# Weights, transposed tokens and tokens by segment laid out on the host, with the layout steps on the chip taken out, in a gated mix of recurrent and local attention

## The chip, the core and the metric

The kernel runs on one core of a Trainium2 chip. The engines named here are PE (TensorE: matrix products; its weight loads are listed apart as PEld), DVE (VectorE), ACT (ScalarE), POOL (GpSimd) and SP (SyncE, which here only issues DMAs; "SPq" and "ACTq" are the queues in which SP and ACT issue them). The metric is the device time of one execution in microseconds, as the median of three runs.

## The reference

The output is a mix of two attentions over the same 2048 tokens of width 640: A is recurrent over 64 segments of 32 tokens, B is local with a window of 8 keys at every second position. All tensors are bf16.

```python
# A: 32 heads of 192, 8 memory tokens, 64 segments of 32 tokens
mem = mem0
for s in range(64):
    h = concatenate([mem, x[:, 32 * s:32 * s + 32]], axis=1)          # 40 tokens
    q, k, v = (einsum('btd,dhe->bhte', h, W) for W in (Wq, Wk, Wv))
    p = softmax(where(mask, q @ k.T * 192 ** -0.5, -1e9))             # causal over the segment, memory open
    o = einsum('bhte,hed->btd', p @ v, Wo)
    mem, a_s = o[:, :8], o[:, 8:]
a = concatenate(a_s)
# B: 32 heads of 20; position t sees t, t-2, ..., t-14
q, k, v = split(x @ wqkv);  b = softmax(q . k_window * 20 ** -0.5) @ v_window @ wo
g = sigmoid((x * gate_w).sum(-1))
out = g * a + (1 - g) * b
```

[...]

## The kernel before

The program has four stages, one after the other.

*Part B* (`part_b`, L87) computes B and the gate g for all tokens and leaves (1 - g) * B in `bsc_dram`. Tokens are in sixteen tiles of 128. `load_x` brings a tile in as rows (ACT issues the first four, POOL the others), `make_xT` (L158) transposes four tiles on PE against an identity (L163; 80 of these, and five more for the memory tokens), copies them from PSUM with DVE or ACT, computes the gate of the four tiles, and has POOL build two more layouts of the same tokens: `xh_blk` (each segment's transposed tokens with the last eight first) and `zx_blk` (the last eight tokens of each segment). `store_blocks` (L200) writes them to `xh_dram` and `zT_dram`, which the later stages read.

The attention of B runs over five blocks of up to 484 tokens and eight head groups of four heads. For each block `proj` (L236) projects q and k in ten chunks of 128 columns and stores each to DRAM (L248), and `load_qk` (L250) loads them back in eight loads with the heads on the partitions that the score products need (the tiles bqT and bkT; 20 rows for each head at partitions 0, 32, 64 and 96). `scores` (L258) and `values` (L280) do a step of one block and one head group. `store_ot` (L303) and `load_ot` (L310) take the block's result (OT) through DRAM again, from 20 rows a head in 32-partition places to dense rows (OTc), for `out_tile` (L318), which multiplies by wo. While a step of one block runs, `fill` gives PE the next block's projections, V products and transposes and the out tiles of the block before, by the lists in `plans`. The last three out tiles are "padded": head groups 6 and 7 are taken from OT as it stands, with a copy of wo that has zero rows in the 12 unused places of each head (`wop`), so that they needn't go through DRAM.

The order of PE, ACT, DVE and SP in this stage is written out by hand (`manual_schedule`). SP issues nearly every DMA. Between the loads and stores of B it issues, by `fetch` (L352), two lists of work for the later stages, one or two entries at a step: first `load_early` (L523) for 13 slices of A's weights that stay on chip, then `copy_scratch` (L527) for 21 half slices that are streamed later: these go from the weight inputs to scratch tensors `wscr` in DRAM, in the order in which the stream needs each row. `sources` (L451) gives the pieces of a slice: a half slice of Wq or Wk is 64 of each 128 columns, a slice of Wv comes in two pieces, one of Wo in rows of 384 or 256 columns.

[...]

*The pre-pass* (`prepass`, L598) computes q, k and v of the last eight tokens of each segment, through all of A's weights, into `zpk_dram`. It loads zT (L609, on ACT's queue) and POOL makes a second layout of it, zTi (L610). Then 48 chunks of q and 48 of k (L621, five products each), for which `get_columns` loads the columns that aren't on chip into the seven slots `wst` (L594), and three rounds of V (L652). `load_late(0)` loads slices of k into place at the beginning of the stage (`wlate_k`, L520, on SP), and some of v at chunks 8 and 17 of k. The results are copied from PSUM by ACT and DVE (ZS, ZV) and stored in rows of some 256 bytes.

*Part A* (`part_a`, L701) is the recurrence: 64 segments, most in a loop. In each, 21 half slices (5 MB) are streamed from `wscr` into the seven slots by `pump` (L553), in the order of `STREAM`, and the other slices are resident.

*The tail* (`part_z`, L1170) makes the last output rows.

`weights_setup` (L500) sorts the slices that are not streamed: the first N_EARLY, which are q slices, are loaded in part B, those after them up to LATE0 bytes a partition in `load_late(0)`, the rest in `load_late(1)`.

Of the kernel before, what the change touches and what calls it, by code (L numbers as in the profile page):

```python
# [15 lines left out]
N_EARLY = 13  # L16
N_LAST = 7
LATE0 = 84992
# [5 lines left out]

def _ap(base, dims):
    return bass.AP(tensor=base.tensor, offset=base.offset, ap=[list(base.ap[0])] + [list(d) for d in dims])

class _K:

    def __init__(self, ctx, tc, A_x, A_mem0, A_Wq, A_Wk, A_Wv, A_Wo, seg_len, B_wqkv, B_wo, gate_w, out):  # L30
# [56 lines left out]
    def part_b(self):  # L87
# [6 lines left out]
        self.zT_dram = self.dram.tile([128, KC, S // 32, 8], BF, name="zT_dram")  # L94
        self.oz_dram = [self.dram.tile([S // 32, 128, 192], BF, name=f"oz_dram{h}") for h in range(2)]
        g_dram = self.dram.tile([4, 32, self.NT], F32, name="g_dram")
        self.xh_dram = self.dram.tile([S // 32, 128, KC * 32], BF, name="xh_dram")
        self.gZ = self.const.tile([128, 4], F32, name="gZ")
        with ExitStack() as ctx:
            wp = ctx.enter_context(tc.tile_pool(name="b_w", bufs=1))  # L100
            io = ctx.enter_context(tc.tile_pool(name="b_io", bufs=4))
            blkp = ctx.enter_context(tc.tile_pool(name="b_blk", bufs=1))
# [8 lines left out]
            self.build_ident(wp)  # L111
            xs = {}

            def load_x(i):
                xs[i] = io.tile([128, 640], BF, name="x_sb")
                (nc.scalar if i < 4 else nc.gpsimd).dma_start(xs[i][:], self.x2d[i * 128:(i + 1) * 128, :])

            for i in range(4):
                load_x(i)
            mem = wp.tile([128, 640], BF, name="mem_sb")  # L120
            nc.vector.memset(mem[:], 0.0)
            nc.sync.dma_start(mem[0:8, :], self.mem0)
# [3 lines left out]
            wqk = [wp.tile([128, KC, 640], BF, name=f"w{n}_sb") for n in "qk"]  # L126
# [4 lines left out]
            wsrc = self.wqkv.rearrange("(c p) f -> p c f", p=128)  # L131
            for n, w in enumerate(wqk):
                (nc.scalar, nc.sync)[n].dma_start(w[:], wsrc[:, :, 640 * n:640 * n + 640])
            nc.sync.dma_start(gw[:], self.gate_w.rearrange("(c p o) -> p c o", p=128, o=1))
            nc.scalar.dma_start(wv[:], wsrc[:, :, 1280:1920])
            nc.sync.dma_start(woc[:], self.wo.rearrange("(c p) f -> p c f", p=128))
            wop = wp.tile([128, 2, 640], BF, name="wo_pad")
            nc.gpsimd.memset(wop[:], 0.0)
            for hh in range(4):
                nc.sync.dma_start(wop[32 * hh:32 * hh + 20], self.wo[480:640].rearrange("(g h d) f -> h d g f", g=2, h=4)[hh])  # L140
# [17 lines left out]
            def make_xT(b, kcs=range(KC)):  # L158
                t0 = 512 * b
                for kc in kcs:  # L160
                    ps = bank(BF, "ps_xT")
                    for i in range(4):
                        nc.tensor.transpose(ps[:, i * 128:(i + 1) * 128], xs[4 * b + i][:, kc * 128:(kc + 1) * 128],  # L163
                                            self.ident[:])
                    self.evac(xT[:, kc, HALO + t0:HALO + t0 + 512], ps[:, 0:512], "act" if b < 2 and kc % 2 else "dve")
                if kcs[-1] < KC - 1:
                    return
                for i in range(4):
                    del xs[4 * b + i]
                    if 4 * b + 4 + i < self.NT:  # L170
                        load_x(4 * b + 4 + i)
# [12 lines left out]
                xv = xT[:, :, HALO + t0:HALO + t0 + 512].rearrange("p c (s t) -> p s c t", t=32)  # L184
                xh = blkp.tile([128, 16, KC, 32], BF, name="xh_blk")
                nc.gpsimd.tensor_copy(xh[:, :, :, 8:32], xv[:, :, :, 0:24])
                s0 = int(b == 0)
                nc.gpsimd.tensor_copy(xh[:, s0:, :, 0:8], xv[:, s0:, :, 24:32])
                if b == 0:
                    ps = bank(BF, "ps_mT")  # L190
                    for kc in range(KC):
                        nc.tensor.transpose(ps[:, kc * 128:(kc + 1) * 128], mem[:, kc * 128:(kc + 1) * 128], self.ident[:])
                    nc.vector.tensor_copy(xh[:, 0, :, 0:8], ps[:, 0:640].rearrange("p (c i) -> p c i", i=128)[:, :, 0:8])
                zx = blkp.tile([128, KC, 16, 8], BF, name="zx_blk")
                nc.gpsimd.tensor_copy(zx[:].rearrange("p c s i -> p s c i"), xv[:, :, :, 24:32])
                blocks[b] = xh, zx

            blocks = {}

            def store_blocks(b):  # L200
                xh, zx = blocks.pop(b)
                self.first_store = nc.sync.dma_start(self.xh_dram[16 * b:16 * b + 16].rearrange("s p f -> p s f"),
                                  xh[:].rearrange("p s c t -> p s (c t)")).ins
                nc.sync.dma_start(self.zT_dram[:, :, 16 * b:16 * b + 16, :].rearrange("p c s i -> p c (s i)"),
                                  zx[:].rearrange("p c s i -> p c (s i)"))
# [30 lines left out]
            def proj(b, n, c):  # L236
# [6 lines left out]
                for kc in range(KC):  # L243
                    nc.tensor.matmul(ps[:, 0:nn], lhsT=wqk[n][:, kc, 128 * c:128 * c + 128], rhs=xT[:, kc, o0:o0 + nn],
                                     start=(kc == 0), stop=(kc == KC - 1))
# [72 lines left out]
            def out_tile(ti, padded=False):  # L318
# [27 lines left out]
            make_xT(0)  # L346
# [3 lines left out]
            bulk = [(self.load_early, k) for k in self.early] + [(self.copy_scratch, k) for k in STREAM]  # L350

            def fetch(n):  # L352
                for f, k in bulk[:n]:
                    f(k)
                del bulk[:n]
# [5 lines left out]
            store_blocks(0)  # L361
            make_v(0, range(2))
            make_xT(1)

            def fill(what):
                for w in what:
                    if w[0] == "x":
                        make_xT(*w[1:])
# [9 lines left out]
            def plan(b, sizes, extra):  # L378
# [3 lines left out]
            x = [[("x", b, (0, 1)), ("x", b, (2, 3)), ("x", b, (4,))] for b in range(4)]  # L382
            o = [("o", i) for i in range(self.NT)]
            plans = [plan(1, (2, 2, 2, 2, 2, 1, 1, 2), ((), (), (), (), (), (), x[2][:1], x[2][1:])),
                     plan(2, (2, 3, 3, 2, 1, 1, 1, 1), ((), (), (), (), (), (), x[3][:1], x[3][1:])),
# [3 lines left out]
            for i, (b, g) in enumerate(steps):  # L389
# [8 lines left out]
                if b < 3 and g == 1:  # L398
                    store_blocks(b + 1)
# [859 lines left out]
```

## Time and profile before

| what | value |
|---|---|
| runs of the kernel | 1607.84, 1609.91 and 1611.03 us, median 1609.91 |
| the profiled execution: its own time, and the span of its trace | 1610.99 and 1609.2 us |
| part B | 0 to 231.5 us |
| pre-pass: q, then k, then V | 231.5 to 283.4, to 347.7, to 408.6 us |
| first segments, and the segment loop | 408.6 to 467.6, to 1522.1 us |
| last segment and tail | 1522.1 to 1609.2 us |

The span is the trace's own length, from its first to its last instruction. Engine shares on the page are means over it. A line of the timeline gives the start, the busy time, the engine, the line of the code, the operation with output and inputs, its shape and how many were grouped; in brackets stands how long the engine had been idle and what ended that.

### The profile page before, as it was taken

What the parts mean: (1) busy time and instruction counts of PE and PEld (TensorE: products, weight loads), DVE (VectorE), ACT (ScalarE), POOL (GpSimd) and SP (SyncE); (2) the same over time, 40 slices, a digit from 0 to 9 for tenths busy, and PEclk for the clock granted to TensorE, in tenths of its full rate; (3) what the DMA queues carried; (4) which work ended last, traced back from release to release, by engine and by line L of the source; (5) the groups of instructions that cost most, each with busy time, mean ns of one, the idle gap of its engine ahead of it and who ended that gap; (6) DMA issues with size and microseconds to landing.
All of it is one profiled execution on the core that took longest, in us unless ns stands there. A gap on an engine that the chain in (4) does not pass through costs nothing. (4 is left out here: it accounts for less than half of the span.)

```text
span 1609.2 us, 91207 instructions
## 1 busy us (share of the span) xinstructions
PE 1473.4 (92%) x36821; PEld 825.0 (51%) x36821; DVE 817.3 (51%) x2249; ACT 656.4 (41%) x1698; POOL 219.2 (14%) x440
## 2 busy tenths in 40 slices
PE   6879579988689999999999999999999999999978
PEld 4434334433345555555555555555555555555557
DVE  3656333322345555555555655555555555555520
ACT  3567442212234444444434434444434444444430
POOL 3100020001011111111111111111111111111100
PEclk9889689989899999999999999999999999999989
DMA  8777839989979999999999999999999999999980
GB/s 219 162 189 178 179 103 285 259 200 278 289 255 334 327 317 333 328 322 339 327 319 328 329 326 333 320 327 333 319 328 319 318 323 335 325 316 331 311 224 16
DMA packets 449581, 454.74 MB, mean 283 GB/s; under 512 B 190144, under 2 KB 315768, under 8 KB 449512
## 3 DMA queue, kind: packets, MB, share of 16 engines
q1 hardware_dynamic: 347912, 405.90, 79.1%
q10 hardware_dynamic: 88992, 26.45, 7.3%
q0 software_dynamic: 12608, 21.45, 4.4%
q8 instruction: 46, 0.75, 0.2%
q14 instruction: 23, 0.19, 0.0%
HBM read 411.95 MB, written 46.82 MB: 285 GB/s over the span
## 5 line engine op out<-in xcount | busy, mean ns | idle before, releaser
L826 ACT CAST aP<-psx 128x512 bf16<-128x512 f32 x128 | 68.7, 589 | 354.1 <-PE psx L819 331.6
L981 PEld LDWEIGHTS <-aP 128*32 128x32 bf16 x6144 | 163.4, 97 | 66.0 <-ACT aP L960 19.6
L917 PE MATMUL psm<-wlate_v,aHa 128*32 128x512 bf16 x2048 | 189.1, 381 | 0.3 <-issue 0.3
L819 PEld LDWEIGHTS <-aHa 128*32 128x32 bf16 x4608 | 115.8, 96 | 116.7 <-PE psm L819 16.8
L981 PE MATMUL psm<-wlate_oa,aP 128*32 128x384 bf16 x2560 | 168.7, 331 | 0.0
L841 DVE STREAM_TRANSPOSE aK<-aP 128x512 bf16<-128x512 bf16 (+1 forms) x256 | 135.0, 546 | 6.9 <-ACT aP L826 0.2
L981 PE MATMUL psm<-wst,aP 128*32 128x384 bf16 (+1 forms) x896 | 121.9, 307 | 9.0 <-DMA wst<-wscr 9.0
L819 PE MATMUL psm<-wres_q,aHa 128*32 128x512 bf16 x1280 | 117.8, 381 | 10.7 <-ACT aK L826 4.6
L981 PE MATMUL psm<-wlate_ob,aP 128*32 128x256 bf16 x2688 | 126.1, 274 | 0.8 <-issue 0.8
L819 PE MATMUL psx<-wlate_k,aHa 128*32 128x512 bf16 x1152 | 118.4, 380 | 0.0
L960 DVE CAST aP<-psx 128x128 bf16<-128x128 f32 (+2 forms) x192 | 75.5, 421 | 84.3 <-PE psx L948 84.1
L838 DVE STREAM_TRANSPOSE aP<-aP 128x512 bf16<-128x512 bf16 (+1 forms) x128 | 74.1, 579 | 85.6 <-ACT aP L826 85.6
L917 PE MATMUL psm<-wlate_v,aHb 128*32 128x512 bf16 x1152 | 115.7, 380 | 0.0
L926 ACT CAST aP<-psm 128x256 bf16<-128x256 f32 (+1 forms) x192 | 86.0, 448 | 49.9 <-PE psS L871 47.0
L819 PEld LDWEIGHTS <-aHb 128*32 128x32 bf16 x3072 | 73.6, 96 | 62.4 <-issue 0.7
L960 ACT CAST aP<-psS 128x384 bf16<-128x384 f32 (+2 forms) x192 | 65.1, 374 | 75.0 <-PE psx L948 50.9
L757 POOL DMA_DIRECT2D aVz<-zpk_dram x64 | 34.8, 544 | 434.4 <-PE psm L819 302.7
L819 PE MATMUL psx<-wst,aHa 128*32 128x512 bf16 x512 | 88.0, 381 | 0.2 <-DMA wst<-wscr 0.2
L273 ACT ACTIVATE bP<-ps_bS 128x968 bf16<-128x968 f32 (+1 forms) x80 | 64.0, 848 | 40.2 <-PE ps_bS L268 39.4
L917 PEld LDWEIGHTS <-aHa 128*32 128x32 bf16 x2304 | 54.5, 96 | 46.0 <-issue 16.0
L819 PE MATMUL psx<-wlate_k,aHb 128*32 128x512 bf16 x768 | 77.9, 383 | 0.0
L750 POOL DMA_DIRECT2D aK<-xh_dram x63 | 34.2, 542 | 321.0 <-PE psm L917 278.8
(177 smaller groups left out, 3235.9 us busy)
## 6 DMA issues: line engine op xcount, KB each, us to landing
wst<-wscr SPq DMA_DIRECT2D x965, 256.0 KB, 4.6
wst<-wscr SPq DMA_DIRECT2D x384, 192.0 KB, 3.8
aP<-zpk_dram SPq DMA_DIRECT2D x64, 192.0 KB, 4.0
zpk_dram<-ZS ACTq DMA_DIRECT2D x5, 2048.0 KB
aVz<-zpk_dram POOLq DMA_DIRECT2D x64, 96.0 KB, 4.3
wres_q<-in_A_Wq_dram SPq DMA_DIRECT2D x10, 512.0 KB
wlate_k<-in_A_Wk_dram SPq DMA_DIRECT2D x8, 512.0 KB
wst<-in_A_Wk_dram SPq DMA_DIRECT2D x14, 256.0 KB
```

What stands on the lines that cost most here:

```text
L273: nc.scalar.activation(Pv, ps[0:nk, :, 0:nq * nu], ACT.Exp, scale=scale_b)
L750: nc.gpsimd.dma_start(xh, row(self.xh_dram, s))
L757: nc.gpsimd.dma_start(vz[:], row(self.zpk_dram, s)[:, 768:1152])
L819: burst([nc.tensor.matmul(pq[32 * j:32 * j + 32, :], lhsT=hT[kc], rhs=sl[j], start=(kc == 0), stop=(kc == KC - 1), tile_position=(0, 32 * ...
L826: nc.scalar.copy(st[i], pqs[i])
L838: nc.vector.transpose(P[p][:, 1:5, c0:c1, :].rearrange("p b c i -> p c b i"), x)
L841: nc.vector.transpose(KT[:, c0:c1, :].rearrange("p c k -> p (c k)"), x)
L917: burst([nc.tensor.matmul(pvs[t][32 * j:32 * j + 32, :], lhsT=hT[kc], rhs=sl[j], start=(kc == 0), stop=(kc == KC - 1), tile_position=(0, 3 ...
L926: (nc.vector.tensor_copy if t == 0 else nc.scalar.copy)(Px[t][:, cs], pvs[t][:, cs])
L960: (nc.scalar.copy, nc.vector.tensor_copy)[g](x.rearrange("p (j c q) -> p j c q", j=2, q=32), pairs[g][:, :, 0:240].rearrange("p j (c q) -> ...
L981: ms.append(nc.tensor.matmul(pso[part][32 * jj:32 * jj + 32, 0:n], lhsT=oT_slot(R // 2, j, 3 * (R % 2) + t), rhs=self.o_weights(osl, part, ...
```

## The change

Three things are done. A function `_lay_out` in numpy, which is run on the host, makes further inputs out of the given ones: every slice of A's weights as a dense block of 128 rows, the tokens transposed (xT), the tokens by segment (xh), the last eight tokens of every segment (zT), wqkv and wo by chunks, and the padded wo. On the chip the identity, the transposes, the memory-token load, POOL's block copies, `store_blocks`, `copy_scratch` and `sources` are gone; each slice is one load from the tensor of slices, and the stream reads the half slices from there. N_EARLY is 15 and LATE0 76800: the resident slices of q are all loaded in part B, and the sets of k and v slices loaded later are as before.

Third, the end of part B is put together in another way. Head groups 0 to 4 of the last block go through DRAM, after step 5 (`store_ot(b, 0, 5)`), and groups 5 to 7 are taken as they stand: tile 12, which lies across two blocks, from a tile `last` into which POOL copies the columns of the block before and DVE those of the last block. All four last out tiles are padded ones, of 14 products each, in the order 13, 14, 15, 12.

In the generated order of instructions, two loads have another place. zT's load on ACT, which stood before the activations of the last four out tiles, stands behind them. The first seven `wst` loads of the pre-pass, which stood in part B between 112 and 190 us, are issued on SP in the first microseconds, four of them before `load_qk(0)`. ACT issues the five wq loads, wv, xT of two blocks and wop before its first evacuation.

```diff
-N_EARLY = 13
+N_EARLY = 15
-LATE0 = 84992
+LATE0 = 76800
...
+def _lay_out(inputs):
...
+    for k in at:
+        half, w = _is_half(k), _width(k)
+        if k[0] in "qk":
+            t = W[k[0]][k[2]][:, 2048 * k[1]:2048 * k[1] + 2048]
+            if half:
+                t = t.reshape(128, 16, 128)[:, :, 64 * k[3]:64 * k[3] + 64]
...
+        flat[at[k]:at[k] + 128 * w] = t.reshape(-1)
...
-            for i in range(4):
-                load_x(i)
...
+            load_xT(0, nc.sync, 0, 128)
+            for c in range(KC):
+                for n in range(2):
+                    (nc.scalar, nc.sync)[n].dma_start(wqk[n][:, c], self.laid["wqk"][n, c].rearrange("p (k f) -> p k f", k=KC))
+            load_xT(0, nc.sync, 128, 512)
+            nc.scalar.dma_start(wv[:], self.laid["wv"])
+            nc.sync.dma_start(gw[:], self.laid["gw"].unsqueeze(2))
+            load_xT(1, nc.sync)
+            load_xT(2, nc.scalar)
+            self.first_store = nc.sync.dma_start(woc[:], self.laid["wo"]).ins
+            load_xT(3, nc.scalar)
+            nc.scalar.dma_start(wop[:], self.laid["wop"])
...
-            def make_xT(b, kcs=range(KC)):
+            def gates(b):
...
-                                  for c, n in ((0, 128), (1, 128), (2, 128), (3, 96))]
-                        pieces += [(OTb[(nb - 1) % 2][:, g, t0:t0 + 128], wop[:, g - 6, fs]) for g in (6, 7)]
+                                  for c, n in ((0, 128), (1, 128), (2, 128), (3, 16))]
+                        own = last[:] if t0 < 0 else OTb[(nb - 1) % 2][:, 5:8, t0:t0 + 128]
+                        pieces += [(own[:, g, :], wop[:, g, fs]) for g in range(3)]
...
-            bulk = [(self.load_early, k) for k in self.early] + [(self.copy_scratch, k) for k in STREAM]
+            bulk = list(self.early)
...
+                if b + 1 == nb and g == 5:
+                    store_ot(b, 0, 5)
+                    o0 = shape_of(b)[2] % 128
+                    nc.gpsimd.tensor_copy(last[:, :, 0:o0], OTb[(b - 1) % 2][:, 5:8, BQ - o0:BQ])
                 if b + 1 == nb and g == 6:
-                    store_ot(b, 0, 6)
                     load_ot(b, 0, 384)
-                    load_ot(b, 384, 480)
-                if g in ((0, 3, 4, 6, 7) if b else (3, 7)):
-                    fetch(1 if len(bulk) > 21 else 2)
+                    load_ot(b, 384, 400)
+                if (g in (0, 3, 4, 6, 7) if b else g in (3, 7)):
+                    fetch(1)
             values(*steps[-1])
-            store_ot(nb - 1, 6, 8)
-            load_ot(nb - 1, 480, 512)
-            load_ot(nb - 1, 512, 640)
+            nc.vector.tensor_copy(last[:, :, o0:128], OTb[(nb - 1) % 2][:, 5:8, 0:128 - o0])
...
-            for ti in range(13, self.NT):
+            for ti in (13, 14, 15, 12):
                 out_tile(ti, True)
-            out_tile(12)
...
     def load(self, key, t):
-        for d, s in self.sources(key, t):
-            self.nc.sync.dma_start(d, s)
+        self.nc.sync.dma_start(t, self.packed[key])
...
-    def copy_scratch(self, k):
-
-        scr = self.dram.tile([128, self.width(k)], BF, name=f"wscr{STREAM.index(k)}")
-        for d, src in self.sources(k, scr[:]):
-            self.nc.sync.dma_start(d, src)
-        self.wscr[k] = scr[:]
...
-                nc.scalar.dma_start(zT[:], self.zT_dram[:].rearrange("p c s i -> p c (s i)"))
+                nc.scalar.dma_start(zT[:], self.laid["zT"])
```

More of the change, by code (lines that the diff above doesn't have):

```diff
@@ L125, in part_b @@
             woc = wp.tile([128, KC, 640], BF, name="wo_sb")
-            wqk = [wp.tile([128, KC, 640], BF, name=f"w{n}_sb") for n in "qk"]
+            wqk = [wp.tile([128, KC, KC, 128], BF, name=f"w{n}_sb") for n in "qk"]
             xT = wp.tile([128, KC, HALO + S], BF, name="xT")
@@ L183, in make_xT @@
                                         op0=ALU.mult, op1=ALU.add)
[L184 to L205, printed above, removed]
             nb = S // BQ + 1
@@ L484, in v_columns @@
         out = []
-        for k in self.parts(("v", t, kc)):
+        for k in _parts(("v", t, kc)):
             sl = self.get_slice(k)
-            out += [sl[:, f:f + 512] for f in range(0, self.width(k), 512)]
+            out += [sl[:, f:f + 512] for f in range(0, _width(k), 512)]
         return out
@@ L501, in weights_setup @@
         nc, tc = self.nc, self.tc
-        rest = [k for u in self.slice_keys() for k in self.parts(u) if k not in STREAM]
+        rest = [k for u in _slice_keys() for k in _parts(u) if k not in STREAM]
         first = ["q", "k", "v", "oa", "ob"]
@@ L512, in weights_setup @@
         self.res_tiles = {}
-        self.wscr = {}
+        at = _places()[0]
+        self.packed = {k: self.laid["slices"][n:n + 128 * _width(k)].rearrange("(p f) -> p f", p=128) for k, n in at.items()}
+        self.wscr = self.packed
         self.wstream = self.ctx.enter_context(tc.tile_pool(name="wstream", bufs=1))
@@ L539, in load_late @@
         place = [k for k in ks if k not in first] + first
-        tiles = {k: pool.tile([128, self.width(k)], BF, name="wlate_" + "_".join(map(str, k))) for k in place}
+        tiles = {k: pool.tile([128, _width(k)], BF, name="wlate_" + "_".join(map(str, k))) for k in place}
         for k in ks:
@@ L1253 @@
         args.append(nc.dram_tensor(f"out_{i}_dram", shape, dt, kind="ExternalOutput").ap())
+    laid = {}
+    for name, a in _lay_out(inputs).items():
+        arrays[f"in_{name}_dram"] = a
+        laid[name] = nc.dram_tensor(f"in_{name}_dram", a.shape, _mybir.dt.from_np(a.dtype), kind="ExternalInput").ap()
     with _tile.TileContext(nc) as tc:
-        kernel(tc, *args)
+        kernel(tc, *args, laid)
     r = _run(nc, [arrays], core_ids=[0])
```

174 lines of the change are left out of this document (78 added, 96 removed).

## The prediction

> **What bounds the kernel now.** I read the page first, for the engine shares, then the busy time by stage, then the timeline and the waits inside each stage that the change touches. From the page:
>
> ```profile
> span 1609.2 us, 91207 instructions
> ...
> PE 1473.4 (92%) x36821; PEld 825.0 (51%) x36821; DVE 817.3 (51%) x2249; ACT 656.4 (41%) x1698; POOL 219.2 (14%) x440
> ```
>
> TensorE (PE) is busy 92% of the span. So only the 136 us in which it is idle, and work that leaves PE, can be won. Where they lie is told by the windows view, one row for each stage (the cuts are at first scores, block starts, first pre-pass product, its V products, the first segment and the loop). Columns: window, length, busy time of each engine, granted clock, DMA share, GB/s.
>
> ```profile
> core 0: us, PE busy (x) PEld busy (x) DVE busy (x) ACT busy (x) POOL busy (x), PEclk, DMA share, GB/s
> 0.00:26.71 26.71, 15.25 (x161) 11.60 (x161) 7.04 (x26) 6.12 (x14) 10.40 (x31) 1.00 0.73 205
> 26.71:53.38 26.67, 23.15 (x279) 12.34 (x279) 17.11 (x45) 11.30 (x36) 5.36 (x7) 0.99 0.87 198
> 53.38:95.00 41.62, 32.29 (x426) 16.35 (x426) 26.45 (x45) 25.88 (x38) 6.83 (x9) 0.83 0.78 169
> 95.00:137.00 42.00, 33.90 (x408) 17.44 (x402) 23.10 (x40) 27.74 (x41) 2.30 (x9) 0.85 0.72 187
> 137.00:175.35 38.35, 28.62 (x406) 15.10 (x404) 23.78 (x41) 27.53 (x41) 3.09 (x12) 0.96 0.79 173
> 175.35:214.65 39.30, 25.73 (x358) 13.77 (x358) 18.76 (x29) 26.18 (x39) 3.84 (x11) 0.63 0.65 151
> 214.65:231.53 16.88, 9.48 (x55) 5.49 (x47) 2.90 (x5) 2.39 (x5) 6.54 (x5) 0.64 0.59 167
> 231.53:283.40 51.87, 51.87 (x241) 23.54 (x242) 15.89 (x23) 14.04 (x24) 0.54 (x1) 1.00 0.95 236
> 283.40:347.68 64.28, 54.02 (x242) 23.79 (x241) 17.27 (x32) 13.85 (x24) 0.00 (x0) 0.92 0.91 222
> 347.68:408.61 60.93, 54.29 (x241) 23.72 (x240) 18.04 (x34) 11.91 (x22) 7.73 (x37) 0.97 1.02 269
> 408.61:467.59 58.98, 41.96 (x1068) 23.49 (x1072) 19.84 (x60) 14.96 (x44) 5.43 (x10) 0.86 0.86 266
> 467.59:1522.05 1054.46, 1031.04 (x30996) 584.60 (x30992) 609.18 (x1830) 455.13 (x1343) 164.98 (x305) 1.00 0.98 326
> 1522.05:1609.20 87.15, 71.85 (x1980) 53.78 (x1972) 17.95 (x40) 19.32 (x30) 2.18 (x4) 0.92 0.51 134
> ```
>
> Two kinds of stage are seen. The segment loop (1054.46 us, 61 periods of 17.29) has PE busy for 98% and a DMA share of 0.98: it has no idle time to give, and the change alters nothing in it but the tensor that the stream is read from. Part B, up to 231.53, leaves PE idle for 63.1 us (231.53 less 168.42 busy), and the pre-pass 17 us. The gain must come from these two, which are also where the removed work stood. Inside part B the timeline shows PE's waits (start, busy us, engine and line, in brackets the idle time before and what ended it):
>
> ```profile
> 26.71 0.25 PE L268 MATMUL ps_bS<-bqT,bkT 20*63 20x56 bf16 x5
> ...
> 83.24 0.78 PE L163 MATMUL ps_xT<-ident,x_sb 128*128 128x128 bf16 x8 [1.03 <-DVE bV L76]
> 86.97 0.68 PE L163 MATMUL ps_xT<-ident,x_sb 128*128 128x128 bf16 x8
> 90.01 0.38 PE L163 MATMUL ps_xT<-ident,x_sb 128*128 128x128 bf16 x4 [2.36 <-DVE xT L76]
> 118.61 2.85 PE L333 MATMUL ps_bo<-wo_sb,OTc 128*128 128x320 bf16 x10 [6.60 <-DMA OTc<-ot_dram]
> 175.35 0.28 PE L268 MATMUL ps_bS<-bqT,bkT 20*128 20x121 bf16 x1 [6.39 <-DMA bkT<-bk_dram]
> 178.27 0.28 PE L268 MATMUL ps_bS<-bqT,bkT 20*128 20x121 bf16 x1 [1.24 <-DMA bkT<-bk_dram]
> 197.08 1.25 PE L333 MATMUL ps_bo<-wo_sb,OTc 128*128 128x320 bf16 x4 [5.69 <-DMA OTc<-ot_dram]
> 221.38 1.25 PE L333 MATMUL ps_bo<-wo_sb,OTc 128*128 128x320 bf16 x4 [6.54 <-DMA OTc<-ot_dram]
> ```
>
> All the long ones are loads of a store-and-load round trip through DRAM (OTc after the values, bkT after the projections). SP, which issues both halves, and the DMA engines have the scratch copies between them:
>
> ```profile
> 165.05 3.36 SPq L254 DMA_DIRECT2D bqT<-bq_dram  x4
> ...
> 171.82 7.00 SPq L531 DMA_DIRECT2D wscr<-in_A_Wk_dram  x1
> ...
> 192.88 0.38 SPq L313 DMA_DIRECT2D OTc<-ot_dram  x1
> 193.31 5.17 SPq L531 DMA_DIRECT2D wscr<-in_A_Wv_dram  x8
> ...
> DMA packets 11133, 2.28 MB, mean 163 GB/s; under 512 B 10368, under 2 KB 11086, under 8 KB 11132
> ```
>
> The last row is the DMA view of 172 to 186 us: 10368 of 11133 packets are under 512 bytes, and 163 GB/s were moved while the loop's stage moved 326.
>
> **The change part by part.** The sum is made against the profiled execution (its own time is 1610.99, span 1609.2; the median of the runs is 1609.91, 1.1 below).
>
> *Start.* No transposes stand ahead of the projections, but all of x, wv, wo and the padded wo now go into the two rings first: 2.62 MB of xT, 4 x 0.82 MB of weights and 0.49 MB of wo padding, 6.4 MB by the tensors' sizes, against 4.1 MB before (four x tiles, the same weights). Four 256 KB pre-pass slices follow on SP ahead of load_qk(0). ACT issues six of the loads before it takes its first k evacuation; behind it stand the bk stores, and behind these the scores.
>
> ```profile
> DMA packets 3365, 3.34 MB, mean 278 GB/s; under 512 B 760, under 2 KB 3365, under 8 KB 3365
> ...
> 22.33 1.50 SPq L254 DMA_DIRECT2D bqT<-bq_dram  x4
> 23.92 1.51 SPq L254 DMA_DIRECT2D bkT<-bk_dram  x4
> ```
>
> The first row is 1 to 13 us. At its 278 GB/s, 7.4 MB are through 26.6 us after 1 us, and the loads' issue to first scores took 4.4 us (22.33 to 26.71): 32 to 36 us, a loss of up to 9. If the stores needn't wait for the rings, the first projection comes earlier by the 20 transposes ahead of it, 2 us by the x8 row above (0.78). The traffic's rate decides, and it is nearer to the loop's 326 GB/s (large rows): 7.4 MB in 22.7 us, part of it behind the stores: first scores at about 29, **+2.5** (-2 to +9). Block 0's transposes themselves are worth nothing here: they stand in the wait for that round trip.
>
> *Part B from block 1.* The 20 transposes of the next block that stand at the end of a block go, with their 1.03 + 2.36 us of waits and their evacuations; the stretch from 83.24 to 90.39 also holds scores, so of its 7 us I take **-4.5** (0 if the DVE evacuations were covering other waits, -6 at most). The 21 copies go, and the pre-pass loads go to the start, so a load_ot or load_qk finds an empty queue. The same transfers without a queue are shown at the start: 22.33 to 26.71, 4.4 us for two loads of four, against 165.05 to 175.35, 10.3 us. So of OTc's 6.60 some 4 go (4 of a 10 us round trip is queueing), of its 5.69 some 5 (copies stood ahead of its stores and eight pieces right behind its load), of bkT's 6.39 + 1.24 some 7: **-16** (-3, if the round trips hold nearly all of it, to -20). Sum of both **-20.5**. POOL's block copies and eight stores of x and z go without effect on the path: POOL is busy for 38 of 231 us. A slice by itself is one 512 KB load now, and 15 of them fill what the copies leave; if they collide with a store, the wait returns at that place, and the low bound has it.
>
> *Turn to the pre-pass.* In before, zT was asked for early:
>
> ```profile
> 214.49 0.35 ACTq L609 DMA_DIRECT2D zT<-zT_dram  x1
> 219.94 4.72 POOL L610 COPY zTi<-zT 128x2560 bf16<-128x2560 bf16 x1 [3.21 <-DMA zT<-zT_dram]
> 231.53 0.39 PE L621 MATMUL ps_pre<-zT,wres_q 128*128 128x512 bf16 x1 [0.70 <-DVE bo L339]
> ```
>
> It took 5.4 us (214.49 to 219.94), hidden under the out tiles. After the change the load stands on ACT behind the last four output activations and the stores that free their buffers. What is late next is PE's first product: the load goes out about when PE ends its last tile, once the store of the tile before has freed a buffer, and takes 5.4 us and its signal: 6.2 in the place of 0.70, +5.5. Ten more matmuls (56 for the last four tiles for 46) are 10 x 0.31 (the row of 221.38: 1.25 for 4), half of them under the wait that is left, 1.5 us. The 6.54 wait shrinks to about 3.2, as only groups 0 to 4 pass through DRAM, two steps earlier. -3.4 + 1.5 + 5.5 = **+3.7** (-2 if the zT load lands under the tiles; +9 if it waits for tile stores too).
>
> *Pre-pass.* PE needs 51.87 / 241 = 0.215 us for a product when nothing is late, so 52 us for each of three equal stages; the k stage took 64.28, the V stage 60.93.
>
> ```profile
> 285.24 0.39 PE L621 MATMUL ps_pre<-zT,wst 128*128 128x512 bf16 x1 [1.09 <-DMA wst<-in_A_Wk_dram]
> ...
> 328.68 0.61 PE L621 MATMUL ps_pre<-zT,wst 128*128 128x512 bf16 x1 [9.17 <-DMA wst<-in_A_Wk_dram]
> ...
> SPq L520 <- DMA zpk_dram<-ZS: 19.5, 2, 10.1
> DVE ZV L76 <- DMA zpk_dram<-ZV: 17.8, 4, 5.9
> ```
>
> The 9.17 arises because SP's late loads waited for ZS stores (19.5 us in two waits) ahead of the wst loads. Every resident q slice is loaded in part B now, so two slices leave that list, seven wst slices are there from the start, and the wst loads that k needs first stand behind V loads only. 9.17 + 1.09 go, and the 1.94 us by which the k stage's products run longer than the q stage's (54.02 - 242 x 0.215): -10.5, cut for a remainder. In the V stage DMA share is 1.02: V slices came in pieces of 256 to 768 bytes and come whole now, but the ZV stores stay: -3.5 of the 9.0 above the floor (0 to -9). Sum **-14** (-3 to -21).
>
> [...]
>
> *Segments and tail.* The stream reads the same rows of 2 KB from an input instead of scratch: 0. The first segments (58.98 us, 3 periods of 17.29 and 7 more) keep their loads: 0 (-5 to +5).
>
> Sum: 2.5 - 20.5 + 3.7 - 14 = -28.3; 1610.99 - 28.3 = 1582.7 for a profiled execution, **1581.6** for the median.
>
> **The rivals.**
>
> *The stream gets slower* (the other side). In the loop PE and DMA are both at 98%; nothing hides a later slice. 61 periods x 17.29 us: 1% longer is 10.5 us, 2.7% (0.46 us a period) eats all of the gain, and 5% gives 1581.6 + 52.7 = 1634. For it: the DMA share of 0.98, and that all slices lie now in one tensor, which no row of this trace shows being read at the loop's rate. Against: rows, sizes and queue are the same, and the inputs came at 278 GB/s in the first 13 us beside small packets.
>
> *Round trips, not queues.* Then OTc and bkT wait as before: part B gives -4.5 alone, and the 6.54 stays (+3.4). 2.5 - 4.5 + 7.1 - 14 = -8.9: 1601. For it: the wait that ended at 197.08 holds 4.2 us from its own load's issue at 192.88, no more than the 4.4 at the start.
>
> [...]
>
> *The pre-pass stays bound by its stores.* ZS and ZV stores are untouched, and where they fill the engines the late loads come no sooner: -2 in the place of -14: 1593.6. For it: DMA share 0.91 to 1.02 there, and DVE's 17.8 us behind ZV stores.
>
> *All waits go.* Start 0, part B -26, turn 0, pre-pass -21: -47: 1563. For it: the copies' small packets are most of part B's.
>
> *The front costs more.* Start +9 and turn +9, the rest as forecast: -16.5: 1593. For it: two orders that put a load ahead of, or behind, what PE needs.
>
> **How the numbers follow.** My forecast 0.41; stream slower 0.06; round trips 0.17; pre-pass bound 0.13; all go 0.14; front 0.09. The forecast's own range is 1572 to 1591; 1558 to 1603 takes in all but the slow stream and tails of the low case and the round trips, some 0.15 to 0.2. About 3 us (0.2%) is what a measurement of this kernel tells from none, as the three runs lie 3.2 apart. Faster by more: all cases but the slow stream, less a tail of the round trips that meets a costly front: 0.92. Of the rest 0.03 lies within 0.2%, and 0.05 is slower.
>
> **What would show it.** First scores at 27 to 31 us; waits for OTc and bkT of 0 to 3 us; no PE row of L163; first pre-pass product at about 217 us (231.53 + 2.5 - 20.5 + 3.7) with a zT wait of 4 to 6 us ahead of it; the k stage at 53 to 55 us, the V stage at 57; the loop's period at 17.29. I am wrong if the period moves by over 0.1 us, if the waits in part B stay above 5 us with an empty queue, or if the wst wait reappears in the k stage.

## The result, and the profile after

The changed kernel took 1590.97 us in the median of four runs (1588.16 to 1598.66), beside 1608.88 for four runs of the kernel before: a ratio of 0.9895 (95% interval 0.9857 to 0.9933), 17.9 us less. In a later comparison on one chip it was 1585.0 beside 1607.55, 0.9873 (0.9838 to 0.9909). The forecast was 1582, in a range of 1558 to 1603.

The first profile is of the longest of its runs (1598.66, span 1597.0), so the second one (span 1583.2) stands beside it here. Times are stage lengths in us; those of the second profile and of the experiments are cut at the same instructions.

| stage | before | after | after, second profile | forecast change |
|---|---|---|---|---|
| start, to first scores | 26.71 | 31.99 | 33.37 | +2.5 |
| first scores to first pre-pass product | 204.82 | 192.89 | 187.39 | -16.8 |
| pre-pass, q | 51.87 | 54.59 | 53.95 | 0 |
| pre-pass, k | 64.28 | 52.15 | 52.64 | -10.5 |
| pre-pass, V | 60.93 | 61.56 | 60.80 | -3.5 |
| first segments | 58.98 | 58.66 | 57.74 | 0 |
| 61 periods of the loop | 1054.46 | 1057.67 | 1048.81 | 0 |
| last segment and tail | 87.15 | 87.49 | 88.50 | 0 |

Up to the loop the change won 15.8 us in one profile (451.84 for 467.59) and 21.7 in the other (445.89), of the 28.3 that were forecast. The loop differs by 8.9 us between two profiles of the same kernel, with the same 30996 products, and lies on both sides of before's. This is the larger part of the spread of the runs, and none of it is the change's as far as these profiles tell.

The windows view of the changed kernel's first profile, in the columns of the one shown of before (of part B, the start, block 0 and the last 24 us):

```profile
0.00:31.99 31.99, 12.46 (x115) 9.19 (x115) 4.46 (x18) 3.69 (x10) 2.15 (x19) 0.89 0.82 257
31.99:59.80 27.81, 23.09 (x258) 11.60 (x259) 12.65 (x39) 11.20 (x36) 0.00 (x0) 0.88 0.52 130
...
201.00:224.88 23.88, 13.99 (x76) 6.12 (x77) 4.82 (x9) 4.82 (x9) 3.21 (x8) 0.69 0.40 128
224.88:279.47 54.59, 54.16 (x236) 24.19 (x241) 15.90 (x23) 14.07 (x24) 4.72 (x1) 0.95 0.64 191
279.47:331.62 52.15, 51.71 (x236) 23.40 (x240) 17.25 (x32) 13.68 (x24) 0.00 (x0) 1.00 0.98 248
331.62:393.18 61.56, 53.82 (x236) 23.80 (x240) 18.04 (x34) 12.11 (x22) 7.76 (x37) 0.94 0.98 268
...
451.84:1509.51 1057.67, 1035.88 (x30996) 584.80 (x30992) 609.62 (x1830) 454.98 (x1343) 165.59 (x305) 1.00 0.97 325
```

Behind the start, DMA share in part B has fallen (0.52 and 0.40 in the rows shown; the start itself went from 0.73 to 0.82), so full DMA engines are an unlikely cause of the waits left there. The k stage is at its floor: PE is busy for 51.71 of its 52.15 us. The V stage is as long as before with a DMA share of 0.98. The timeline of the same profile shows the waits that are left:

```profile
31.99 0.88 PE L292 MATMUL ps_bS<-bqT,bkT 20*63 20x56 bf16 x8 [2.80 <-DMA bkT<-bk_dram]
59.80 0.28 PE L292 MATMUL ps_bS<-bqT,bkT 20*128 20x121 bf16 x1 [4.67 <-DMA bkT<-bk_dram]
122.02 2.85 PE L358 MATMUL ps_bo<-wo_sb,OTc 128*128 128x320 bf16 x10 [4.47 <-DMA OTc<-ot_dram]
172.23 0.40 PE L292 MATMUL ps_bS<-bqT,bkT 20*128 20x121 bf16 x7 [0.70 <-DMA bkT<-bk_dram]
175.53 3.00 SPq L332 DMA_DIRECT2D ot_dram<-OT  x4
182.34 0.39 SPq L337 DMA_DIRECT2D OTc<-ot_dram  x1
186.49 2.85 PE L358 MATMUL ps_bo<-wo_sb,OTc 128*128 128x320 bf16 x10 [4.26 <-DMA OTc<-ot_dram]
205.96 1.36 PE L358 MATMUL ps_bo<-wo_sb,OTc 128*128 128x320 bf16 x4 [2.02 <-DMA OTc<-ot_dram]
218.12 0.34 ACTq L580 DMA_DIRECT2D zT<-in_zT_dram  x1
224.88 0.59 PE L592 MATMUL ps_pre<-zT,wres_q 128*128 128x512 bf16 x1 [6.16 <-DMA zT<-in_zT_dram]
```

bkT's 6.39 + 1.24 us in block 4 are down to 0.70. OTc's 6.60 and 5.69 are still 4.47 and 4.26, and 6.54 became 2.02. In block 4 the round trip of OTc is laid open: stores from 175.53, the load at 182.34, the product at 186.49, 11 us with nothing else on SP between 175 and 190. The 6.16 us for zT are new.

### The profile page after: what moved, and what is told of

It is laid out like the page before. It is cut to its first block, busy times and chain, and to the rows that moved or that the text cites. A ratio compares the mean times of both kernels' runs of the same rounds, so it can differ in the third digit from the quotient of the medians.

```text
span 1597.0 us, 90910 instructions
## 1 busy us (share of the span) xinstructions
PE 1472.0 (92%) x36731; PEld 817.9 (51%) x36746; DVE 806.5 (50%) x2231; ACT 653.8 (41%) x1694; POOL 200.8 (13%) x415
## 5 line engine op out<-in xcount | busy, mean ns | idle before, releaser
L790 PE MATMUL psx<-wlate_k,aHa 128*32 128x512 bf16 x1152 | 121.7, 384 | 0.0
L790 PE MATMUL psm<-wres_q,aHb 128*32 128x512 bf16 x1024 | 79.0, 382 | 0.0
```

What stands on the lines that cost most here:

```text
L790: burst([nc.tensor.matmul(pq[32 * j:32 * j + 32, :], lhsT=hT[kc], rhs=sl[j], start=(kc == 0), stop=(kc == KC - 1), tile_position=(0, 32 * ...
```

## The experiments

Twelve runs followed, the first of them of the changed kernel itself. Since the loop's length differs by some 9 us from profile to profile, small effects are read from stage lengths.

**The kernel again.**

> The changed kernel itself, for a second profile and more times. The profile of it that is there is of its longest run (1598.66 us against 1588 to 1593 in the three others). If the 3.2 us by which its segment loop is longer than before's (1057.67 against 1054.46 us) belong to that run alone, this profile has a loop of 1052 to 1056 us and a span near 1589. If the stream is slower from the input tensor for good, the loop is 1057 us again.

It is the second profile of the table: 1585.0 us in the median, loop 1048.81, which is below the 1052 to 1056 expected. So a stream that is slower for good is not seen, and the 3.2 us lie within what the loop varies by: over all the profiles of the changed kernel and its variants the loop took from 1048.8 to 1057.7 us.

**zT's load ahead of the last tiles.**

```diff
-            io = ctx.enter_context(tc.tile_pool(name="b_io", bufs=1))
+            io = ctx.enter_context(tc.tile_pool(name="b_io", bufs=1, side="right"))
```

> One pool (the buffers of B's output tiles) lies at the other end of on-chip memory, so that zT no longer takes over their place; its load then stands ahead of the last four output activations. My theory: the wait of 6.16 us ahead of the first pre-pass product goes to under 1 us, and the slow products after it (about 2 us) with it: pre-pass start 5.5 us earlier against the end of part B, total 6 to 8 us under the changed kernel. Rival: something else is late next (a ZS buffer, a slice) and less than 2 us come through.

1578.12 us in the median, 0.9813 of before (0.9781 to 0.9846), 6.9 under the changed kernel in the same comparison. Its timeline:

```profile
201.42 0.34 ACTq L580 DMA_DIRECT2D zT<-in_zT_dram  x1
...
216.08 0.39 PE L592 MATMUL ps_pre<-zT,wres_q 128*128 128x512 bf16 x1 [0.70 <-DVE bo L364]
```

The load goes out 14.7 us ahead of its use, the wait is 0.70 as in before, and the first product takes 0.39 us in the place of 0.59. The q stage is 51.81 us in the place of 53.95 and 54.59. The late load of zT thus cost 5.5 us of waiting and 2.1 to 2.8 of slow products: the theory's 6 to 8.

The wait isn't steady either. In the kernels that leave zT's load in its place it took from 4.91 us (the next run) to 10.89 (the transposes). From the issue of zT's load to the first product it was 6.8 us in the changed kernel's first profile (218.12 to 224.88), where SP had begun to send its late k slices 0.6 us ahead of that load (217.53), and 7.3 in the kernel with the transposes (219.38 to 226.68), where it had begun 5.8 us ahead (213.55). No run moved the slices alone, so whether they slow the load is not shown. These differences are part of the times below.

**The scratch copies back.**

```diff
-            bulk = list(self.early)
+            bulk = [(self.load_early, k) for k in self.early] + [(self.copy_scratch, k) for k in STREAM]
...
-                    fetch(1)
+                    fetch(1 if 21 < len(bulk) <= 32 else 2)
```

> The changed kernel with the 21 scratch copies put back, in the same small pieces from the weight inputs, and the stream read from scratch. Theory of queues (mine): the waits for bkT and OTc in blocks 3 and 4 return, +8 to +15 us in part B. Theory of round trips: the waits in blocks 3 and 4 stay as they are in the changed kernel within 3 us, and total moves by less than 4. For the loop: 1054 us if scratch is read faster than the input tensor, no difference to the changed kernel's own second profile if not.

1602.69 us in the median, 17.7 over the changed kernel in the same comparison; up to the loop its profile is 9.3 and 15.2 us longer than the changed kernel's two (461.10 for 451.84 and 445.89). The edit also issues the first four of the 15 resident slices two at a time. The stretch from block 2's first out tile to block 4's tile that waits for OTc holds most of the copies. The windows view of that stretch, in the usual columns, of before, of the copies put back, and of the changed kernel:

```profile
118.61:197.08 78.47, 57.77 (x760) 31.31 (x761) 42.98 (x73) 51.12 (x75) 6.21 (x20) 0.80 0.81 183
```

```profile
123.81:197.56 73.75, 55.91 (x761) 30.58 (x761) 42.86 (x73) 51.45 (x75) 6.86 (x21) 0.85 0.77 171
```

```profile
122.02:186.49 64.47, 52.62 (x760) 29.12 (x761) 42.76 (x73) 51.19 (x75) 7.13 (x21) 0.92 0.65 169
```

The copies are worth 9.3 us there (73.75 for 64.47), within the 8 to 15 of the theory of queues. The kernels that leave this stretch alone took from 64.2 to 66.5 us in it, so 7 to 9.5 is what can be put down to the copies. PE's own busy time is 3.3 us of the difference: the same 760 products took 55.91 us at a granted clock of 0.85, and 52.62 at 0.92. But the kernel with the wst loads later, without copies, has 55.84 us at 0.88, so that part isn't shown to be the copies'. With the copies, block 4's longest waits are 2.46 us for bkT and 7.04 for OTc:

```profile
175.29 0.23 PE L292 MATMUL ps_bS<-bqT,bkT 20*128 20x121 bf16 x1 [2.46 <-DMA bkT<-bk_dram]
197.56 2.85 PE L358 MATMUL ps_bo<-wo_sb,OTc 128*128 128x320 bf16 x10 [7.04 <-DMA OTc<-ot_dram]
```

OTc's wait has come back, and of bkT's 6.39 + 1.24 only a part (with the shorter ones 4.79 us in four waits, where before has 9.26).

The loop, streamed from scratch, took 1049.58 us, inside the spread of the variants that stream from the input: no difference between the two sources is seen.

**Stores of a block's result one step earlier.**

```diff
-                if b > 0 and g == 1:
+                if b > 0 and g == 0:
                     store_ot(b - 1, 0, 8)
```

> The stores of a block's result (OT) are issued one step earlier, at the end of step 0 of the next block; nothing else is moved. Theory of round trips: the waits of 4.47 and 4.26 us for OTc are the length of store and load less the three steps between, so a step of some 3.5 us earlier leaves under 1 us of each: 5 to 8 us less in total. Theory of queues: OTc arrives when the queue lets it, and the waits stay above 3 us.

OTc's wait in block 2 fell to 1.92 us, the one in block 4 stayed at 4.51. The time was 1587.79 us, no change that the runs can tell (the changed kernel: 1585.0). Neither theory had it: in block 4 the stores had been waiting for the last values and not for their place in SP's order, so a place one step earlier is worth nothing there. From first scores to the pre-pass it took 184.13 us, 3.3 under the shorter of the changed kernel's two profiles, of which 1.25 are a shorter zT wait (4.99); so block 2 may have won some 2 us, too little for the medians.

**Out tiles one step later.**

```diff
-((), (), (), (), o[0:1], o[1:2], o[2:3], o[3:4])
+((), (), (), (), (), o[0:1], o[1:2], o[2:3])
...
-[o[6:7], o[7:8], (), (), o[8:9], o[9:10], o[10:11], o[11:12]]
+[o[6:7], o[7:8], (), (), (), o[8:9], o[9:10], o[10:11]]
...
+            out_tile(11)
             for ti in (13, 14, 15, 12):
```

> The out tiles that need a block's freshly loaded OTc stand one step later, and tile 11 behind the last values, ahead of the padded tiles. Theory of round trips: OTc is loaded some 11 us after its last values whatever the queues hold, so one more step of work (3.5 us) ahead of it takes the waits of 4.3 us to under 1.5 us, and tile 11 fills the wait of 2 us at the end; 6 to 9 us less before the pre-pass. Rival: the steps are bound by ACT, so work taken out of them only leaves holes elsewhere, and the pre-pass begins less than 3 us earlier.

```profile
120.66 1.52 PE L358 MATMUL ps_bo<-wo_sb,OTc 128*128 128x320 bf16 x10 [1.22 <-DVE bV L140]
...
184.09 2.85 PE L358 MATMUL ps_bo<-wo_sb,OTc 128*128 128x320 bf16 x10 [2.82 <-DMA OTc<-ot_dram]
```

In this timeline the wait in block 2 is gone (1.22 us for DVE is left) and the one in block 4 is 2.82. From first scores to the pre-pass it took 187.25 us, where the changed kernel's two profiles have 192.89 and 187.39: the expected 6 to 9 us are not shown. The runs spread from 1576.19 to 1594.75 (median 1590.96).

**Late loads taken out of the start.**

```diff
-            load_xT(2, nc.scalar)
...
-            load_xT(3, nc.scalar)
-            nc.scalar.dma_start(wop[:], self.laid["wop"])
...
+                if (b, g) in ((0, 2), (0, 5)):
+                    load_xT(2 + int(g == 5), nc.sync)
+                if (b, g) == (1, 2):
+                    nc.sync.dma_start(wop[:], self.laid["wop"])
```

> xT of the last two blocks and the padded wo, 1.8 MB, go out within part B (SP, steps 2 and 5 of block 0 and step 2 of block 1) and not in ACT's ring ahead of the first evacuation. If the start is late because ACT stands behind these issues and the rings' bytes (my step for the start), first scores come at 26 to 28 us and not at 31.7 to 33.4. [...]

```profile
25.94 0.56 PE L289 MATMUL ps_bS<-bqT,bkT 20*63 20x56 bf16 x5
...
59.71 2.58 PE L246 MATMUL ps_bv<-wv_sb,xT 128*128 128x320 bf16 x9 [14.49 <-DMA xT<-in_xT_dram]
```

First scores come at 25.94 us, 6.1 and 7.4 earlier than in the changed kernel's profiles (30.87 to 33.37 in all the kernels that leave the start alone): the 1.8 MB in the rings were the loss at the start. But a V product of block 1 then waited 14.49 us for xT, and the time was 1595.28.

**The same loads between ACT's evacuations.**

```diff
             load_qk(0)
+            load_xT(2, nc.scalar)
+            load_xT(3, nc.scalar)
+            nc.scalar.dma_start(wop[:], self.laid["wop"])
```

> xT of the last two blocks and the padded wo are issued by ACT between its first k evacuations, so that ACT no longer stands behind them, and early enough that no V product waits for xT as one did (14.49 us) where they were sent within block 0. Mine: first scores at 27 to 30 us (25.9 with these loads out of the way, 31.7 to 33.4 with them ahead), and the gain kept to block 1 (first scores there at 55 to 57 and not 60 us). Rival: the bytes fill the rings all the same, and first scores stay at 31 us or later.

First scores at 31.32 us, block 1's at 60.72, 1588.47 in all: the rival. ACT was free early here (its table load stands at 4.94 us, 10.84 in the changed kernel), yet nothing came sooner. The two combined kernels below, which begin in the same way, had first scores at 28.68 and 30.16 us, so 1 to 3 us may be had by it, hardly clear of the spread. The larger part is that these loads are ahead of the stores, and not ACT's standing behind the issues: in the changed kernel's first profile SP's stores of q and k waited 6.1 us for loads of xT to land (three waits, the longest 2.2). Whether it is the loads' bytes or something else that holds them up was not told apart. Its time has 2.2 us more of waiting for zT (8.43).

**The wst loads later.**

```diff
-            self.first_store = nc.sync.dma_start(woc[:], self.laid["wo"]).ins
+            nc.sync.dma_start(woc[:], self.laid["wo"])
...
+                if b == 1:
+                    self.first_store = dma.ins
```

> The seven wst loads of the pre-pass (1.8 MB) are let out after the stores of block 1's result and not in the first microseconds. If they hold up the first loads of q and k, first scores come 2 to 4 us earlier than 31.7 to 33.4; if the rings' other bytes decide, by under 1.5 us. The k stage of the pre-pass tells also whether the early wst loads have to do with the 12 us that it lost: 52 us again if the cause is the order of the k loads, over 60 us if the early loads were it.

In the changed kernel SP issues these seven loads between 14.98 and 31.46 us. Without them there, first scores came at 30.33 us, 0.5 below the earliest of the kernels that leave the start alone, block 1's at 55.22 (59.80 and 60.00 in the changed kernel's two profiles), the first out tile at 115.63 (122.02 and 119.13). That tile had waited 6.05 us for OTc. Then the lead is given back: the stretch from there to block 4's tile took 67.60 us at a granted clock of 0.88, against 64.2 to 66.5 in the kernels that leave it alone, zT's wait was 7.61, and the time is 1590.86. So of before's 78.47 us in that stretch 1 to 3 may be the wst loads among the copies, hardly clear of the spread; the change moved them to the start and did not win them. The k stage took 52.89 us: the early wst loads are not what shortened it.

**Transposes back.**

```diff
+                for kc in kcs:
+                    ps = bank(BF, "ps_xT")
+                    for i in range(4):
+                        nc.tensor.transpose(ps[:, i * 128:(i + 1) * 128], woc[:, kc, 128 * i:128 * i + 128], self.ident[:])
+                    self.evac(scr[:], ps[:, 0:512], "dve")
```

> The 40 transposes and their ten evacuations on DVE stand at the ends of blocks 0 and 1 again, where before had them for the last two blocks of tokens; they transpose wo into a tile that nothing reads. My forecast put their removal at 4.5 us (0 to 6) in all. Mine: the time from first scores to block 2's first out tile (90.0 us in the changed kernel, 91.9 before) rises by 4 to 6 us. Rival: they fill waits that are there anyway (bkT's in block 1), and it rises by under 2.

```profile
88.83 0.78 PE L223 MATMUL ps_xT<-ident,wo_sb 128*128 128x128 bf16 x8 [1.03 <-DVE bV L140]
95.59 0.58 PE L223 MATMUL ps_xT<-ident,wo_sb 128*128 128x128 bf16 x4 [2.37 <-DVE xT_again L140]
119.85 2.85 PE L368 MATMUL ps_bo<-wo_sb,OTc 128*128 128x320 bf16 x10 [2.59 <-DVE bP L311]
```

The waits of before are there to within a hundredth (1.03 and 2.37 for 1.03 and 2.36), but from first scores to the first out tile it took 86.55 us, between the 90.03 and 85.76 of the changed kernel's two profiles. No cost is shown; the place where OTc is waited for has 2.59 us for DVE instead of 4.47 for OTc. The time was 1592.0 us (1590.24 to 1595.68); the changed kernel's medians are 1590.97 and 1585.0. In the profile the zT wait of 10.89 us, 4.7 more than in the changed kernel, is a part of it.

**Wo's slices after the V stage.**

```diff
+                if part == 1 and k[0] != "v":
+                    self.after_v.append((k, tiles[k][:]))
+                else:
+                    self.load(k, tiles[k][:])
...
+            for k, t in self.after_v:
+                self.load(k, t)
```

> The slices of Wo that come in during the V stage (some 5 MB) are loaded after that stage. If the V stage (60.8 to 61.7 us in every run so far, before and after) is bound by DMA bandwidth shared with these loads, it falls to 52 to 56 us. If it is bound by the ZV stores' own small rows and the three ZV buffers, it stays above 59 us. The first segments get longer in both cases, as the loads stand there.

This kernel was run once (1594.12 us), and it tells nothing apart. SP issued the loads from 22.7 us into the stage (355.81) where the changed kernel does from 19.3 (350.91), so they stayed in its middle, and the stage took 60.67 us with a DMA share of 1.00. What bounds the V stage wasn't settled. In the changed kernel's first profile the engines that copy its results into ZV waited there for ZV's stores, ACT 24.9 and DVE 8.8 us, and PE waited 5.4 us for the copies: this points to the stores.

**Together.** The next has the zT edit, the later out tiles and the loads between ACT's evacuations; the last also lets the wst loads out after block 1's `load_qk`.

> Three edits together: zT's load ahead of the last tiles, the out tiles a step later, the start's late loads between ACT's evacuations. If the parts add up: pre-pass start at 209 to 213 us (216 with zT alone, 218 with the tiles alone), and 1570 to 1578 us in all. Rival: PE's clock or ACT takes it back, and it is not under zT alone (1578).

> As best4, and the pre-pass's seven wst loads are let out after block 1's loads of q and k. If they held up block 0 and block 1 (first scores of block 1 came at 55.2 us with them late, at 60 with them early), another 2 to 4 us under best4. Rival: they only move their collision to block 1 and 2, as with the stores of block 1's result (OTc's wait 6.05), and best5 is the same as best4 within 3 us.

They took 1574.47 us (0.98 of before, 0.9772 to 0.9828) and 1572.71 (0.9794, 0.9764 to 0.9823), and the pre-pass began at 210.0 and 209.43 us, as expected if the parts add up. They do not differ from each other beyond their intervals: the rival of the last holds, later wst loads gain nothing more. In best5:

```profile
209.43 0.39 PE L595 MATMUL ps_pre<-zT,wres_q 128*128 128x512 bf16 x1 [0.70 <-DVE bo L363]
```

These are the fastest kernels of the study, 2% under before. By time alone they are not told from the kernel with the zT edit by itself (0.9781 to 0.9846 of before), though the pre-pass begins some 6 us earlier than its 216.08.

## Why the prediction was right, and where it was not

The direction, the two places (part B and the pre-pass) and the range held; the gain was 17.9 us at first and 22.6 later, of the 28 forecast. The sum was 28.3, and by its terms:

- *Start*, +2.5 forecast, +5.3 and +6.7 measured, inside its bounds. The loads ahead of the stores were the right cause (25.94 us without 1.8 MB of them). The step that put ACT's wait beside it has little behind it: with ACT free early the scores came at 28.7 to 31.3 us.
- *Transposes*, -4.5 forecast. The DVE waits on which it rests are real and came back with them, but the run that has them shows no loss that it could tell from the spread of 85.8 to 90.0 us. The term was too large.
- *Waits for bkT*, -7 forecast, 7.63 to 0.70: the size is right. That they were queueing behind the copies is shown for a part: with the copies back 2.46 came back. SP began these loads 46.4 us after block 2's first out tile in before, 41.2 with the copies back, and 38.3 in the changed kernel; what else had held them up is open.
- *Waits for OTc*, -9 forecast for two of them, -3.6 measured (6.60 to 4.47, 5.69 to 4.26). Its own sign, waits of 0 to 3 us, was missed. Here the rival of round trips was right: 11 us from the stores to the product with an empty queue. The step that failed is "4 of a 10 us round trip is queueing", which took the start's loads alone, 4.4 us, for what a store and a load need together. Nor were they "the same transfers": the start's eight loads have 35 and 39 KB each, those of block 4 that they were set against 151 and 156 KB. The queue did cost something. In before's timeline (first here) the last values were ready at 182.80, but SP was issuing copies until 185.06; after the change the stores followed the values at once:

```profile
182.09 0.71 DVE L300 TENSOR_TENSOR OT<-ps_bO,b_rz 128x484 bf16<-128x484 f32 x1 [0.43 <-ACT b_rz L298]
185.16 4.31 SPq L308 DMA_DIRECT2D ot_dram<-OT  x4
```

```profile
174.78 0.72 DVE L324 TENSOR_TENSOR OT<-ps_bO,b_rz 128x484 bf16<-128x484 f32 x1 [0.43 <-ACT b_rz L322]
175.53 3.00 SPq L332 DMA_DIRECT2D ot_dram<-OT  x4
```

  From the last values to the product it took 14.3 us before (182.80 to 197.08) and 11.0 in the changed kernel (175.50 to 186.49): 3.3 us were the queue's, 2.4 of them ahead of the stores, and 11 the trip's own, with four stores that SP issues one behind the other.
- *Copies as a whole*: 7 to 9.5 us in that stretch by the run that has them back, 3.3 of it PE's busy time, which the sum had left out.
- *Turn*, +3.7 forecast. The zT wait was as forecast (6.2 foreseen, of which 0.8 for the signal was the author's estimate; 6.16 and 6.24 measured; that it was so near is in part luck, with 4.91 to 10.89 in the variants), and the 6.54 fell to 2.02, a little more than the forecast 3.2. From its first padded product to the pre-pass it took 18.92 us (205.96 to 224.88), before 10.15 (221.38 to 231.53): less the 5.5 of zT, 3.3 for the longer tiles in the place of 1.5 (2.4 in the second profile).
- *k stage*, -10.5 forecast, -12.1 and -11.6 measured: right, and the wst wait is gone. The runs exclude the copies (52.19 us with them back) and the early wst loads (52.89 without them) as its cause. That it is the order of the late loads, as forecast, was not tried by itself, but SP's timeline fits it, before and after:

```profile
300.71 21.18 SPq L520 DMA_DIRECT2D wlate_v<-in_A_Wv_dram  x16
321.98 4.99 SPq L594 DMA_DIRECT2D wst<-in_A_Wk_dram  x5
```

```profile
295.57 5.72 SPq L498 DMA_DIRECT2D wlate_v<-in_slices_dram  x8
301.39 17.08 SPq L565 DMA_DIRECT2D wst<-in_A_Wk_dram  x5
```

  The late V loads, 16 pieces, held the next wst loads back until 38.6 us into the stage, 10.1 us of it in a wait for ZS stores; with eight whole slices they begin 21.9 us into it.
- *V stage*, -3.5 forecast, +0.6 and -0.1 measured. The pieces of the V slices are gone and the stage is as long. Its stores by ACT take more of the DMA engines than its loads do, as the DMA views of the stage show, before and after:

```profile
DMA packets 33353, 16.43 MB, mean 269 GB/s; under 512 B 15896, under 2 KB 32552, under 8 KB 33350
...
q10 hardware_dynamic: 20185, 7.48, 53.1%
q1 hardware_dynamic: 13133, 8.89, 48.8%
```

```profile
DMA packets 25769, 16.54 MB, mean 267 GB/s; under 512 B 15271, under 2 KB 22967, under 8 KB 25766
...
q10 hardware_dynamic: 21731, 7.68, 56.0%
q1 hardware_dynamic: 4003, 8.79, 42.2%
```

  The loads (q1) have a third of the packets and their share falls by 6.6 points; the rate of all stays (269 and 267 GB/s). The term priced the loads' pieces; that the stores set the stage is likely by the waits above and not shown by a run.
- *q stage*, 0 forecast, +2.7 and +2.1 measured: the slow products after the zT wait. The first product took 0.59 us after 6.16 us of waiting, 0.58 after 6.24 in the second profile and 0.39 after 0.70 (with zT's load moved), and the stage got 2.1 to 2.8 us shorter without the wait. Before's k stage had shown the like: 0.61 us for the first product after 9.17 us of waiting, 0.39 after 1.09. The sum has no term for it; it belonged there.
- *Stream*, 0: right as far as the spread tells.

That part B behind first scores came out near its forecast (-11.9 and -17.4 for -16.8) is in part luck. The transposes, the waits and the turn, as measured in the first profile, give only -6.3. Another 5.2 us are the same 760 products running faster between block 2's first out tile and block 4's, a term that the sum did not have. In the second profile the two are -8.1 and 4.8, and 4.5 us are not accounted for.

## What to carry to other kernels

The wait for a round trip through DRAM had two parts here: what its own store and load needed (11.0 us from the last values to the product), and what stood in the queue with them (3.3 us more). Look for the same trip in a stretch with an empty queue, stores included and with transfers of the same size, before the whole wait is put down to the queue. When layout work is taken off the chip, look at what its order had been holding back or letting through: here one load fell behind the last tiles because its place in memory had another tenant, and one changed word (the side of a pool) gave 7 of the 29 us by which that kernel then led over before.

## What the runs showed of the hardware

The granted clock of PE was not the same in part B from kernel to kernel: the same 760 products took 57.77 us at a mean clock of 0.80 in before, and 52.62 at 0.92 in the changed kernel. Of the 14.0 us by which the stretch got shorter (78.47 to 64.47), 5.2 are faster products and not waits. Shorter waits alone don't tell the clock: with the wst loads later, the stretch has a wait of 3.08 us for OTc in the place of 4.26, and yet 55.84 us of products at 0.88. And a loop with the same instructions took from 1048.8 to 1057.7 us from one profile to the next, at a granted clock of 1.00 in the two profiles of the changed kernel; what differs was not found.
